# Fewer and larger stores and halo copies, transposes copied out by two engines, an earlier load of one chunk, and a divided last store in a convolution + Wave-MLP kernel

## The chip, the cores and the metric

The kernel runs on 1 core of one Trainium2 chip. The metric is the device time of one execution in microseconds (us). The engines are PE (matrix multiply, with PEld its weight loads), DVE (vector), ACT (scalar and activation), POOL (which issues the loads of input and weights) and SP (which issues stores, halo copies and row loads). In the timelines below each engine works through its own queue in order (ACT comes to a copy at 39.84 us behind three other operations), and so do the queues of DMA issues (POOL's loads of chunk 3 at 24.30 us behind the weights at 22.03).

## The reference, cut to what matters

```python
# x: (8, 4224, 192), a causal 7-tap convolution per head, then:
theta = x @ w_theta
zr, zi = x * cos(theta), x * sin(theta)
y = einsum('ts,bsd->btd', w_tok_r, zr) + einsum('ts,bsd->btd', w_tok_i, zi)
u = x + y
out = u + maximum(u @ w_ch, 0)
```

The two 4224 x 4224 token matrices are nearly all of the arithmetic. The tokens are made in 33 chunks of 128; the mixing of the first chunks has to start while later ones are still being made.

## The kernel before: the parts that the change touches

A chunk goes through `conv` (PE, from the input window `xw` with 16 rows of history from the chunk before), `transpose` (PE into PSUM tile `tp`, then a copy to `uT`), `theta` (PE, then cosine and sine on ACT), `product` and `sums` (DVE). Only then can PE mix it (`y`), and the results are added into `pv` by DVE or, on the first visit, copied by ACT.

```python
def transposed(uT, u, gs, by_dve=False):
    tp = banks("tp", F16)                      # one PSUM tile for both halves g
    for g in gs:
        for k in range(6):
            pe(nc.tensor.transpose(tp[:, g, k*P:(k+1)*P], u[:, g*GC + k*P : ...], ident))
    g = slice(gs[0], gs[-1] + 1)
    evacuate(uT[...][:, g, :], tp[:, g, 0 : 6*P], by_dve)   # ONE copy, DVE or ACT

class Chunk:
    def __init__(self, k, before=None):
        for a in range(NQ):                    # NQ = 4
            ...
            if before is not None:             # 4 halo copies of 48 KB
                nc.sync.dma_start(out=hist, in_=before.xw[lo + Q : lo + Q + HALO, h, :, :])
            ...
            nc.gpsimd.dma_start(out=self.xw[lo : lo + n, h, :, :], in_=x[:, t0 : t0 + n, :]...)
    def conv(self, j):
        ...
        if j == 1:                             # 4 stores of 96 KB, xs in token order
            for a in range(NQ):
                nc.sync.dma_start(out=xs[t0 : t0 + Q, :], in_=self.x[a*Q : (a+1)*Q, :])
    def transpose(self):
        transposed(self.xT, self.x, range(NG), self.k < 3)  # DVE for chunks 0 to 2, then ACT

def load_x(self, i):                           # x of a row block: one load of 384 KB
    nc.sync.dma_start(out=self.xr[i], in_=xs[self.tbs[i]*P : (self.tbs[i]+1)*P, :])
# ... (cut) ... in the program's start:
steps[0].load_rows()
for m in (1, 2):
    steps[0].load_w(m)       # first token weights, tile st, two buffers
load_chunk(2)
for m in (1, 2):
    steps[1].load_w(m)
for i in range(NW + 2):      # NW = 11
    # conv(i), theta(i-1), load_chunk(i + 3), transpose(i), product and sums of i-1, mixing between
```

## Time and profile before

| kernel before | value |
|---|---|
| time, median of the 4 runs beside the changed kernel | 1448.92 us (1445.77 to 1449.5) |
| span of the profiled execution | 1446.4 us |
| PE busy / PE idle | 1416.3 / 30.1 us |
| PE idle in the first 105 us, by waits | DVE accumulations 5.1 us, ACT copies 3.0 us, one late load 0.9 us |

The prediction shows the busy times, the stretches and PE's waits. These are lines of the timelines (start, duration, engine, line, operation, what it writes and reads, and in brackets the idle time before it and what ended it). An L number is a line of the kernel at hand, so the same statement has another number in another kernel.

```profile
32.85 0.96 DVE L251 TENSOR_TENSOR z<-z 128x1536 f16<-128x1536 f16 x1 [1.57 <-ACT z L246]
...
37.44 0.95 DVE L408 TENSOR_TENSOR pv<-y,pv 128x768 f32<-128x768 f32 x1
```

```profile
34.06 1.50 ACT L151 ACTIVATE uT<-tp 128x1536 f16<-128x1536 f16 x1
```

```profile
18.68 2.29 POOL L323 DMA_DIRECT2D st<-in_moe_w_tok_i_dram  x4
20.96 4.57 POOL L197 DMA_DIRECT2D xw<-in_x_dram  x8
```

DVE's accumulation at 37.44 ends PE's wait of 0.78 us at 38.45, so DVE is close to the path here.

### The profile page before, as it was taken

The numbers are of one execution on the slowest core, as the hardware profiler recorded it, in microseconds if no ns is written. First come the engines' busy times: TensorE is split into PE (matmuls) and PEld (weight loads), VectorE is DVE, ScalarE is ACT, GpSimd is POOL, SyncE is SP. The second block draws the span as 40 slices with busy tenths as digits, with TensorE's granted clock in tenths as the row PEclk, the third lists the DMA queues.
The fourth block names the chain that finished last, engine by engine and source line by source line (L and its number), as shares of the span: only waits on it lengthen the run. The fifth ranks groups of instructions, "written<-read, shape, count | busy, mean of one in ns | idle before, by whom it ended". The sixth has DMA issues, their size and how long they took to land.

```text
span 1446.4 us, 23748 instructions
## 1 busy us (share of the span) xinstructions
PE 1416.3 (98%) x9809; PEld 887.9 (61%) x9809; DVE 979.2 (68%) x1051; ACT 315.5 (22%) x379; POOL 435.1 (30%) x655
## 2 busy tenths in 40 slices
PE   7899999999999999999999999999999999999997
PEld 5556666666666666666666666666666666666665
DVE  6893555545548777866666657877777667767686
ACT  5861101111134254000000004435210110010133
POOL 7431211111233232432433342233323123213120
PEclk9999999999999999999999999999999999999999
DMA  9986756465699998998899989999999999998893
GB/s 173 227 178 145 146 103 149 90 149 97 137 231 219 214 250 217 228 254 183 213 256 213 242 143 245 228 188 234 279 216 206 209 204 221 204 203 194 166 222 125
DMA packets 272029, 281.99 MB, mean 195 GB/s; under 512 B 106672, under 2 KB 240176, under 8 KB 271920
## 3 DMA queue, kind: packets, MB, share of 16 engines
q0 software_dynamic: 162464, 92.15, 48.4%
q1 hardware_dynamic: 71824, 178.88, 35.1%
q10 hardware_dynamic: 37632, 9.44, 4.1%
q8 instruction: 77, 1.26, 0.3%
q14 instruction: 32, 0.26, 0.1%
HBM read 245.49 MB, written 108.13 MB: 244 GB/s over the span
## 4 chain that ended last, share of the span: by engine, by line
PE 89%; DVE 4%; DMA 3%; POOL 2%; ACT 1%; issue 1%; SPq 0%; DVEq 0%; ACTq 0%; POOLq 0%
PE y L443 82%; PE v L141 5%; PE pc L210 1%; PE tp L165 1%; POOL st L323 1%; DMA xw<-in_x_dram 1%; DVE z L257 1%; DVE wt L336 1%; DVE pv L408 1%; ACT z L246 1%; DVE z L251 0%; DVE pv L476 0%; DVE wt L348 0%; POOL xw L197 0%; DMA xs<-z 0%
## 5 line engine op out<-in xcount | busy, mean ns | idle before, releaser
L443 PE MATMUL y<-z,wt 128*128 128x384 f16 x7656 | 1283.6, 326 | 10.6 <-DVE pv L408 7.5
L443 PEld LDWEIGHTS <-wt 128*128 128x128 f16 x7656 | 740.8, 98 | 488.6 <-issue 10.6
L408 DVE TENSOR_TENSOR pv<-y,pv 128x768 f32<-128x768 f32 x324 | 308.9, 954 | 323.6 <-PE y L443 282.8
L336 DVE STREAM_TRANSPOSE wt<-st 128x1408 f16<-128x1408 f16 (+7 forms) x224 | 327.8, 1465 | 48.5 <-PE y L443 39.0
L323 POOL DMA_DIRECT2D st<-in_moe_w_tok_r_dram x232 | 132.5, 578 | 466.1 <-DVE wt L336 461.0
L323 POOL DMA_DIRECT2D st<-in_moe_w_tok_i_dram x232 | 132.7, 578 | 404.4 <-DVE wt L336 388.9
L348 DVE TENSOR_TENSOR wt<-wt 128x1408 f16<-128x1408 f16 (+7 forms) x216 | 176.7, 818 | 40.8 <-PE y L443 38.4
L151 ACT ACTIVATE z<-pc 128x768 f16<-128x768 f32 x65 | 53.2, 819 | 387.2 <-PE pc L210 386.9
L151 ACT ACTIVATE ub<-pv 128x768 f16<-128x768 f32 x63 | 50.2, 835 | 333.0 <-DVE pv L408 310.4
L406 ACT ACTIVATE pv<-y 128x768 f32<-128x768 f32 x66 | 54.0, 819 | 282.0 <-PE y L443 282.0
L141 PEld LDWEIGHTS <-uT 128*128 128x128 f16 x1056 | 91.0, 98 | 25.8 <-issue 7.9
L386 POOL TENSOR_TENSOR pv<-pv,xr 128x1536 f32<-128x1536 f32 x24 | 74.5, 3105 | 68.6 <-DVE pv L476 22.1
L197 POOL DMA_DIRECT2D xw<-in_x_dram x132 | 76.4, 585 | 31.0 <-DMA xw<-xw 8.7
L476 DVE SCALAR_TENSOR_TENSOR pv<-v,pv 128x768 f32<-128x768 f32 x66 | 62.9, 954 | 27.5 <-PE v L141 27.1
L257 DVE TENSOR_TENSOR z<-z 128x768 f16<-128x768 f16 x132 | 73.4, 556 | 3.6
L151 ACT ACTIVATE uT<-tp 128x1536 f16<-128x1536 f16 (+1 forms) x48 | 58.2, 1215 | 74.4 <-PE tp L165 74.4
L246 ACT ACTIVATE z<-v,half_pi 128x768 f16<-128x768 f32 x66 | 59.8, 907 | 41.2 <-PE v L141 40.8
L251 DVE TENSOR_TENSOR z<-z 128x1536 f16<-128x1536 f16 x66 | 60.0, 947 | 7.5 <-ACT z L246 7.5
L141 PE MATMUL v<-wth,uT 128*128 128x192 f16 x528 | 55.0, 248 | 4.4 <-ACT z L246 3.0
L141 PE MATMUL v<-wch,uT 128*128 128x192 f16 x528 | 54.2, 246 | 2.1 <-DVE pv L476 1.2
L246 ACT ACTIVATE z<-v 128x768 f16<-128x768 f32 x66 | 53.4, 809 | 0.0
L210 PE MATMUL pc<-xw,bands 96*64 96x192 f16 x528 | 35.8, 258 | 2.6 <-ACT bands L625 1.1
(44 smaller groups left out, 142.4 us busy)
## 6 DMA issues: line engine op xcount, KB each, us to landing
part<-pv SPq DMA_DIRECT2D x79, 768.0 KB, 4.3
pv<-part SPq DMA_DIRECT2D x79, 768.0 KB, 6.1
out_dram<-pv SPq DMA_DIRECT2D x66, 384.0 KB, 4.3
st<-in_moe_w_tok_r_dram POOLq DMA_DIRECT2D x136, 176.0 KB, 5.5
st<-in_moe_w_tok_i_dram POOLq DMA_DIRECT2D x136, 176.0 KB, 5.1
xs<-z SPq DMA_DIRECT2D x132, 96.0 KB, 4.5
xw<-in_x_dram POOLq DMA_DIRECT2D x121, 96.0 KB, 6.1
xr<-xs SPq DMA_DIRECT2D x24, 384.0 KB, 3.7
```

Of the source, the lines that this page charges most:

```text
L141: pe(nc.tensor.matmul(v[:, k, b * D : (b + 1) * D], lhsT=tT[:, 3 * k + b + i, :], rhs=w[:, 2 * b + i, :], start=(i == 0), stop=(i == 1),))
L151: act(nc.scalar.activation(out=out, in_=in_, func=AT.Copy))
L197: nc.gpsimd.dma_start(out=self.xw[lo : lo + n, h, :, :], in_=x[:, t0 : t0 + n, :].rearrange("b s d -> s b d"),)
L246: act(nc.scalar.activation(**args))
L257: dve(nc.vector.tensor_tensor(out=z[:, o, :], in0=z[:, a, :], in1=z[:, b, :], op=ALU.subtract))
L323: pool(nc.gpsimd.dma_start(out=st[a * Q : (a + 1) * Q, 0:nb, :, 0:n] .rearrange("i r bt s -> i (r bt) s"), in_=w[self.tbs[0] * P : (self.t ...
L336: dve(nc.vector.transpose(self.w[name][:, 0 : self.n, :, :], self.st[int(name[1])][:, int(name[0]) - 1, :, 0 : self.n * Q] .rearrange("p b ...
L348: dve(nc.vector.tensor_tensor(out=self.w[name][:, 0 : self.n, :, :], in0=self.w[a][:, 0 : self.n, :, :], in1=self.w[b][:, 0 : self.n, :, : ...
L386: ins = pool(nc.gpsimd.tensor_tensor(out=self.pv[i], in0=self.pv[i], in1=self.xr[i], op=ALU.add))
L408: dve(nc.vector.tensor_tensor(out=o, in0=yv, in1=o, op=ALU.add))
L443: pe(nc.tensor.matmul(y[cn][:, q, 0:BH], lhsT=self.w[wn][:, c, :, :].rearrange("p bt i -> p (bt i)"), rhs=chunks[k].z[:, zn, q * BH : (q + ...
L476: dve(nc.vector.scalar_tensor_tensor(out=ub, in0=channel_mix(self.uT[i][:, 6 * g : 6 * g + 6, :], wch), scalar=0.0, in1=ub, op0=ALU.max, o ...
```

## The change

The intent: move half of each transpose copy from ACT to DVE where ACT is busy, free SP and the DMA queues of many small issues, have chunk 2's input sooner, and shorten the end.

```diff
-    xs = dram.tile([S, N], F16, name="xs")
+    xs = dram.tile([NK, P, N], F16, name="xs")
 # transposed(): copies by halves, first ACT, then DVE
-        g = slice(gs[0], gs[-1] + 1)
-        evacuate(uT[...][:, g, :], tp[:, g, 0 : 6 * P], by_dve)
+        for g in [slice(g, g + 1) for g in gs] if shared else [slice(gs[0], gs[-1] + 1)]:
+            evacuate(uT[...][:, g, :], tp[:, g, 0 : 6 * P], shared and g.start == 1)
-            transposed(self.xT, self.x, range(NG), self.k < 3)
+            transposed(self.xT, self.x, range(NG), self.k < NW)
 # Chunk: two halo copies of 96 KB for four of 48 KB
+            for lo in (0, WR) if before is not None else ():
+                nc.sync.dma_start(out=self.xw[lo : lo + HALO, :, :, :],
+                                  in_=before.xw[lo + Q : lo + Q + HALO, :, :, :])
 # conv: one store for four
-                for a in range(NQ): ... nc.sync.dma_start(out=xs[t0 : t0 + Q, :], ...)
+                nc.sync.dma_start(out=xs[self.k, :, :], in_=self.x)
 # load_x: four loads of 96 KB for one of 384 KB
+            for j in range(NQ):
+                a, k = divmod(NQ * self.tbs[i] + j, NK)
+                nc.sync.dma_start(out=self.xr[i][j * Q : (j + 1) * Q, :],
+                                  in_=xs[k, a * Q : (a + 1) * Q, :])
 # output, last two of the kernel: ReLU-add and store by halves, on ACT's and SP's queues
+            for k in (slice(0, 1), slice(1, 2)) if last_ones else (slice(0, 2),):
+                dve(nc.vector.scalar_tensor_tensor(out=u[:, k, :], in0=v[:, k, :], ...))
+                dma = nc.scalar.dma_start if last_ones and k.start == 0 else nc.sync.dma_start
 # start of the program
     steps[0].load_rows()
+    load_chunk(2)
     for m in (1, 2):
         steps[0].load_w(m)
-    load_chunk(2)
 # (cut) the channel weights wch are loaded in a later step; the accumulating loads follow xs's new shape
```

More of the change, by code (lines that the diff above doesn't have):

```diff
@@ L133, in token, with x_rows @@
         return (a * NK + k) * Q
+    def x_rows(tb):
+        found = []
+        for j in range(NQ):
+            a, k = divmod(NQ * tb + j, NK)
+            if found and found[-1][2] == a:
+                found[-1][1].append(k)
+            else:
+                found.append((j * Q, [k], a))
+        return [
+            (slice(lo, lo + len(ks) * Q), slice(ks[0], ks[-1] + 1), slice(a * Q, (a + 1) * Q))
+            for lo, ks, a in found
+        ]
     def channel_mix(tT, w):
@@ L158, in crossed, with transposed @@
         act(nc.scalar.dma_start(out=uT, in_=u, transpose=True))
-    def transposed(uT, u, gs, by_dve=False):
+    def transposed(uT, u, gs, shared=False):
         tp = banks("tp", F16)
@@ L168, in transposed @@
                 ))
-        g = slice(gs[0], gs[-1] + 1)
-        evacuate(
-            uT[:, :, :].rearrange("p (g k) s -> p g (k s)", g=NG)[:, g, :],
-            tp[:, g, 0 : 6 * P], by_dve,
-        )
+        for g in [slice(g, g + 1) for g in gs] if shared else [slice(gs[0], gs[-1] + 1)]:
+            evacuate(
+                uT[:, :, :].rearrange("p (g k) s -> p g (k s)", g=NG)[:, g, :],
+                tp[:, g, 0 : 6 * P], shared and g.start == 1,
+            )
     Z11, T1, Z21, Z22, T2, T4, T3 = range(7)
@@ L182, in __init__ @@
             self.xw = wk.tile([2 * WR, 2, B, D], F16, name="xw", tag="big", bufs=6)
+            for lo in (0, WR) if before is not None else ():
+                nc.sync.dma_start(
+                    out=self.xw[lo : lo + HALO, :, :, :],
+                    in_=before.xw[lo + Q : lo + Q + HALO, :, :, :],
+                )
             for a in range(NQ):
@@ L185, in __init__ @@
                 t0 = token(k, a)
-                hist = self.xw[lo : lo + HALO, h, :, :]
                 if before is not None:
-                    nc.sync.dma_start(
-                        out=hist, in_=before.xw[lo + Q : lo + Q + HALO, h, :, :]
-                    )
+                    pass
                 elif t0 == 0:
-                    nc.vector.memset(hist, 0.0)
+                    nc.vector.memset(self.xw[lo : lo + HALO, h, :, :], 0.0)
                 else:
@@ L224, in conv @@
             if j == 1:
-                for a in range(NQ):
-                    t0 = token(self.k, a)
-                    nc.sync.dma_start(
-                        out=xs[t0 : t0 + Q, :], in_=self.x[a * Q : (a + 1) * Q, :]
-                    )
+                nc.sync.dma_start(out=xs[self.k, :, :], in_=self.x)
         def transpose(self):
             self.xT = turned()
-            transposed(self.xT, self.x, range(NG), self.k < 3)
+            transposed(self.xT, self.x, range(NG), self.k < NW)
         def theta(self, g):
@@ L378, in load_x @@
             self.xr[i] = wk.tile([P, N], F16, name="xr", tag="xr", bufs=1)
-            nc.sync.dma_start(
-                out=self.xr[i], in_=xs[self.tbs[i] * P : (self.tbs[i] + 1) * P, :]
-            )
+            for j in range(NQ):
+                a, k = divmod(NQ * self.tbs[i] + j, NK)
+                nc.sync.dma_start(
+                    out=self.xr[i][j * Q : (j + 1) * Q, :],
+                    in_=xs[k, a * Q : (a + 1) * Q, :],
+                )
         def add_x(self, i):
@@ L393, in add_ahead @@
             tb = self.tbs[i]
-            for cols in (slice(0, HN), slice(HN, N)):
-                pool(nc.gpsimd.dma_start(
-                    out=part[which][tb, :, cols], in_=xs[tb * P : (tb + 1) * P, cols],
-                    accum_op=ALU.add,
-                ))
+            for rows, ks, a in x_rows(tb):
+                for cols in (slice(0, HN), slice(HN, N)):
+                    pool(nc.gpsimd.dma_start(
+                        out=part[which][tb, rows, cols].rearrange("(k i) n -> i k n", i=Q),
+                        in_=xs[ks, a, cols].rearrange("k i n -> i k n"), accum_op=ALU.add,
+                    ))
         def give(self, y, i, h, copies):
@@ L473, in output @@
         def output(self, i, g):
-            u = self.pv[i][:, g * GC : (g + 1) * GC]
-            ub = u.rearrange("p (k n) -> p k n", k=2)
-            dve(nc.vector.scalar_tensor_tensor(
-                out=ub, in0=channel_mix(self.uT[i][:, 6 * g : 6 * g + 6, :], wch), scalar=0.0, in1=ub,
-                op0=ALU.max, op1=ALU.add,
-            ))
-            rows = slice(self.tbs[i] * P, (self.tbs[i] + 1) * P)
-            nc.sync.dma_start(
-                out=out[g * GB : (g + 1) * GB, rows, :].rearrange("b s d -> s b d"),
-                in_=u.rearrange("p (b d) -> p b d", d=D),
-            )
+            u = self.pv[i][:, g * GC : (g + 1) * GC].rearrange("p (k n) -> p k n", k=2)
+            v = channel_mix(self.uT[i][:, 6 * g : 6 * g + 6, :], wch)
+            rows = slice(self.tbs[i] * P, (self.tbs[i] + 1) * P)
+            last_ones = self.t == NSTEP - 1
+            for k in (slice(0, 1), slice(1, 2)) if last_ones else (slice(0, 2),):
+                dve(nc.vector.scalar_tensor_tensor(
+                    out=u[:, k, :], in0=v[:, k, :], scalar=0.0, in1=u[:, k, :],
+                    op0=ALU.max, op1=ALU.add,
+                ))
+                b = slice(g * GB + 2 * k.start, g * GB + 2 * k.stop)
+                dma = nc.scalar.dma_start if last_ones and k.start == 0 else nc.sync.dma_start
+                dma(
+                    out=out[b, rows, :].rearrange("b s d -> s b d"),
+                    in_=u[:, k, :].rearrange("p k (b d) -> p (k b) d", d=D),
+                )
         def outputs(self):
@@ L528, in step_events, with load_wch @@
                 found.append((1.3 + 3 * (m - 1), lambda m=m: nxt.load_w(m)))
+        if t == NU - 2:
+            def load_wch():
+                dve(nc.vector.memset(wch[:, 1:3, :], 0.0))
+                for rows, i, part_w in channel_pieces(moe_w_ch):
+                    pool(nc.gpsimd.dma_start(out=wch[rows, i, :], in_=part_w))
+            found.append((3, load_wch))
         for at, f in outputs:
@@ L698 @@
         between(1)
-    dve(nc.vector.memset(wch[:, 1:3, :], 0.0))
-    for rows, i, part_w in channel_pieces(moe_w_ch):
-        nc.gpsimd.dma_start(out=wch[rows, i, :], in_=part_w)
     ready[0] = NK
```

## The prediction

> **What bounds the kernel now.** I read the page first: busy times, then the chain that ended last, then the costliest group.
>
> ```profile
> PE 1416.3 (98%) x9809; PEld 887.9 (61%) x9809; DVE 979.2 (68%) x1051; ACT 315.5 (22%) x379; POOL 435.1 (30%) x655
> PE 89%; DVE 4%; DMA 3%; POOL 2%; ACT 1%; issue 1%; SPq 0%; DVEq 0%; ACTq 0%; POOLq 0%
> L443 PE MATMUL y<-z,wt 128*128 128x384 f16 x7656 | 1283.6, 326 | 10.6 <-DVE pv L408 7.5
> ```
>
> PE is busy 1416.3 of 1446.4 us, and its row also carries 89% of the chain. The token-mix matmuls (L443) are 1283.6 us of it. So the most that any change around PE can win is the 30.1 us in which PE is idle. The listing of instruction order shows that PE's own sequence is the same in both kernels, instruction for instruction: no matmul is added, removed or moved. The question is only which idle stretches of PE shrink or grow. The table of stretches tells where they lie.
>
> ```profile
> 20.00:28.00 8.00, 6.38 (x67) 4.24 (x65) 7.66 (x11) 5.19 (x7) 7.32 (x14) 1.00 1.37 196
> 28.00:39.00 11.00, 7.45 (x71) 4.66 (x67) 9.12 (x17) 8.82 (x11) 5.10 (x9) 0.99 1.32 219
> 39.00:46.00 7.00, 6.61 (x56) 4.34 (x54) 5.48 (x8) 5.56 (x7) 5.63 (x10) 0.77 0.96 133
> 46.00:63.00 17.00, 14.35 (x138) 9.69 (x139) 13.43 (x22) 15.83 (x21) 8.05 (x15) 1.00 1.28 266
> 63.00:82.00 19.00, 18.30 (x176) 12.41 (x176) 17.05 (x26) 17.86 (x24) 4.62 (x9) 1.00 1.05 225
> 82.00:105.00 23.00, 19.65 (x153) 12.70 (x152) 22.45 (x31) 13.07 (x16) 6.71 (x12) 1.00 0.82 178
> 1441.00:1446.40 5.40, 0.00 (x0) 0.00 (x0) 1.01 (x2) 0.00 (x0) 0.00 (x0) 0.89 0.50 169
> ```
>
> Columns: window, length, busy us of PE, PE weight loads, DVE, ACT, POOL, granted clock, DMA share, GB/s. Three limits follow each other in the first 105 us, where chunks are made while the mixing already runs: DMA at 20 to 28 (share over 1), ACT at 46 to 63 (15.83 of 17), DVE at 82 to 105 (22.45 of 23). After 105 PE idles only about 3 us until 1420. At the end 5.4 us pass with no PE work. The waits of PE before 110 us, in the waits view:
>
> ```profile
> PE y L443 <- DVE pv L408: 5.1, 5, 2.5
> PE y L443 <- ACT pv L406: 3.0, 3, 1.2
> PE pc L210 <- DMA xw<-in_x_dram: 0.9, 1, 0.9
> PE v L141 <- ACT uT L151: 0.8, 1, 0.8
> ```
>
> The timeline of PE dates the ones that matter:
>
> ```profile
> 27.70 0.52 PE L210 MATMUL pc<-xw,bands 96*64 96x192 f16 x7 [0.88 <-DMA xw<-in_x_dram]
> 36.31 0.48 PE L443 MATMUL y<-z,wt 128*128 128x384 f16 x2 [1.23 <-ACT pv L406]
> 38.45 0.50 PE L443 MATMUL y<-z,wt 128*128 128x384 f16 x2 [0.78 <-DVE pv L408]
> 46.45 0.83 PE L141 MATMUL v<-wth,uT 128*128 128x192 f16 x8 [0.75 <-ACT uT L151]
> 53.91 0.49 PE L443 MATMUL y<-z,wt 128*128 128x384 f16 x2 [0.61 <-ACT pv L406]
> 63.10 0.48 PE L443 MATMUL y<-z,wt 128*128 128x384 f16 x2 [0.99 <-DVE pv L408]
> 104.61 10.57 PE L443 MATMUL y<-z,wt 128*128 128x384 f16 x64 [2.46 <-DVE pv L408]
> ```
>
> [...]one record of 0.5 lasts 3.41 us from 38.87, just after the idle at 34 to 38. It costs at most 1.7 us. [...]the trace has 0.96. So I take 0.55 us for the new half of 768[...]; the next operation starts about 0.1 us before the end, which leaves 0.45 of DVE time. [...]The last store[...] 2.66 us from issue to landing, of which its 32 packets per engine of 36 ns take 1.15.
>
> **Part by part.**
>
> *Transposes on two engines, chunks 0 to 10.* Before, chunks 0 to 2 were copied whole by DVE (0.96 us), chunks 3 to 10 whole by ACT (about 1.46, next start 1.33 later). Now each is half ACT (0.81, next start 0.69 later; the same shape stands at the end of the trace) and half DVE (0.45). For chunks 3 to 10 ACT loses 0.64 each and DVE gains 0.45 each. On the path: the wait at 46.45 ends 0.65 earlier and the one at 53.91 by another 0.6, as ACT runs back to back there. So PE is about 1.25 us earlier by 58. At 36.31 ACT's saving does not count, because the next wait (38.45) is for DVE. DVE takes its halves for chunks 3 and 5 in idle time (1.57 and 1.81 us before L251). Chunk 6's half lies between L336 at 59.63 and the accumulation that ends the wait at 63.10: 0.45 back. Chunks 7 and 8 fall before an idle of 1.44 at 82.04 and are free. Chunks 9 and 10 fall into the unbroken DVE stretch that ends at 104.6: 0.9 back. About 0.4 more comes from three small ACT waits between 63 and 82. Sum: -1.25 - 0.4 + 0.45 + 0.9 = -0.3 us.
>
> *Chunk 2 loaded before the first weights.* Chunk 2 was not late (its convolution at 20.5 waits for no DMA), and the first weights move 2.3 us later: last landing near 17 instead of 14.7, while DVE needs them done by 19.7, the next transpose. Their eight instructions take 2.6 us, so that just fits. What is gained is indirect: chunk 3's halo copies can now go at about 15 us and no longer compete, at 19.6 to 21.4, with chunk 3's own loads, which land at 27.66 in a stretch with DMA share over 1. 192 KB at the 196 GB/s of that stretch is 1 us; the 0.88 us wait goes, and what follows is ACT-bound up to 38.45. I take -0.6.
>
> *Stores and halos.* Four xs stores of 0.43 us issue become one of about 0.35; four halo copies of 0.53 become two. SP saves about 2.3 us per chunk, but SP is not what PE waits for. New: the loads of x come in four pieces, and the order puts the first set between the xs stores, so SP waits at about 25 for chunk 2's store to land (4 to 5 us). Chunk 4's halos then land near 35 instead of 35.3; its convolution is at 36.7. No cost. Later the 24 loads of x issue some 1.3 us longer each; the additions that need them waited only 2.3 us in all for a load.
>
> *Channel weights later.* A memset of 0.22 leaves DVE's unbroken stretch before 104.6, and four POOL issues leave that region: -0.2.
>
> *End.* The last two ReLU-adds become four halves, each stored on its own.
>
> ```profile
> 1440.19 1.82 DVE L476 SCALAR_TENSOR_TENSOR pv<-v,pv 128x768 f32<-128x768 f32 x2 [0.91 <-PE v L141]
> 1441.17 1.23 SPq L481 DMA_DIRECT2D out_dram<-pv  x2
> ```
>
> The last full one ends at 1442.01, its store lands at 1444.70. Four halves cost DVE about 0.1 more in all; the last store carries 16 packets per engine instead of 32, so 0.58 less, while the other half has gone on ACT's queue 0.45 us before. -0.5.
>
> Sum: -0.3 - 0.6 - 0.2 - 0.5 = -1.6 us. A further -1.5 is possible if the half-clock window vanishes. [...]I count a third of it plus a little for waits that I hold too pessimistically: about -3 us in all.
>
> **The rivals.** (a) *DVE becomes the bound of the whole start.* Then its eight halves, 8 x 0.45 = 3.6 us, less 1.35 saved on chunks 0 to 2, arrive at 104.6: up to +2. For it: 22.45 of 23 us busy from 82, and the largest single wait of PE (2.46) is for DVE. Against: five idle stretches of 1.4 to 1.8 us before 82. Time: about 1450.5. (b) *A wait on SP replaces the ones removed*: x loads placed among the stores hold halos back and a chunk comes late. For it: in-order queue, DMA share over 1. Against: halos run a chunk or more ahead. Time: +2, 1451. (c) *Everything is hidden but the tail*: PE waits for other things at once, -0.5 only: 1448.7. (d) *The starting chain was as ACT- and DMA-bound as it looks* and PE recovers most of its waits and the half clock: -5, 1444.
>
> **Range and chances.** From the median before, 1449.16, less 3: **1446.0 us**. The three runs before spread over 3.7 us (1445.77 to 1449.5), and rivals lie between 1444 and 1451; weighing (a) and (b) at a fifth together, 1442.5 to 1449.8 should hold it eight times in ten. Two per cent is 29 us, which is all of PE's idle time, so faster by over 2% has 0.01; slower by as much would need a stall of that size that nothing in the profile prepares: 0.01.
>
> **What would show it.** PE busy near 1416 us and the same instruction counts. The wait at 27.7 for in_x_dram gone or under 0.3. No PE wait for the ACT transpose copy near 46. DVE busy about 2.3 us more in total, and PE's wait before 105 us still for the accumulation, at 2 us or more. ACT below 14.5 of 17 us in 46 to 63. The last two stores landing 0.5 us nearer to the last DVE instruction. Wrong would be: PE reaching its long unbroken run (104.6 now) later than 105, a new wait for the halo copies or for xs, or a changed idle total between 105 and 1420, which I take to be untouched.

The sum stays at -1.6 us, and at about -3 with a third of 1.5 for the half clock and some 0.9 for waits. What is missing is the working of the 0.55 us for DVE's half copy, from which the 0.45 of the first step comes, so 0.55 stands as the author's guess beside the 0.96 of a whole copy; the trace before shows 0.556 us for DVE's subtractions of 128x768 in f16 (`z<-z`, L257, mean of 132), and the half copies of the changed kernel then took 0.56 (L163). The 1.5 rests on the record alone, 3.41 us at a granted clock of 0.5; what brings such a record about was not shown.

## More of the kernel before

ACT's whole transpose copy starts at 34.06, after DVE's product at 32.85: in this kernel DVE never waits for that copy. And POOL issues chunk 3's loads from 20.96, right behind the second set of weights.

## The result, and the profile after

| | before | after |
|---|---|---|
| time, median of 4 runs | 1448.92 us (1445.77 to 1449.5) | 1461.93 us (1458.39 to 1463.47) |
| ratio of the fast runs, 95% interval | | 1.0091 (1.0067 to 1.0115) |
| span of the profiled execution | 1446.4 us | 1461.2 us |
| PE busy | 1416.3 us | 1421.4 us |
| PE idle | 30.1 us | 39.8 us |

A ratio here is the mean time of one kernel's fast runs over that of the other's of the same rounds, so not quite the ratio of the medians quoted beside it. The change costs about 13 us, or 0.9%: within 2%, but 12 us above the predicted range.

In the profiled executions the span grew by 14.8 us, and that is PE idle +9.7 and PE busy +5.1. The first line is from the page's busy times and the second from its costliest groups (busy us, mean ns of one; idle before it).

```profile
PE 1421.4 (97%) x9809; PEld 889.8 (61%) x9809; DVE 981.3 (67%) x1061; ACT 313.0 (21%) x382; POOL 437.7 (30%) x657
...
L459 PE MATMUL y<-z,wt 128*128 128x384 f16 x7656 | 1287.5, 327 | 14.9 <-DVE pv L424 13.3
```

There are 9809 matmuls as before and in the same order, so a longer busy time points to a slower clock: the mean granted clock is 0.993 in place of 0.998, and the table of stretches below shows where. The idle time before the mixing matmuls for a DVE accumulation went from 7.5 to 13.3 us. The timeline of PE dates the new waits:

```profile
32.03 0.85 PE L226 MATMUL pc<-xw,bands 96*64 96x192 f16 x7 [3.34 <-DMA xw<-in_x_dram]
...
47.16 0.82 PE L459 MATMUL y<-z,wt 128*128 128x384 f16 x2 [4.39 <-DVE pv L424]
...
117.09 5.30 PE L459 MATMUL y<-z,wt 128*128 128x384 f16 x16 [3.24 <-DVE pv L424]
```

Against the same matmuls before (27.70, 38.45 and 104.61), PE is 4.3 us late at 32, 8.7 us late at 47 and 12.5 us late at 117; by 122.5 it is 15.1 us late, and from there to the end the difference stays at 15. Between 47 and 117 it grows mostly in two waits, of 1.19 us for a DVE accumulation at 68.99 and of 1.36 us for ACT at 89.02.

Where the 4.39 us come from is seen on DVE, ACT and PE's transposes together:

```profile
33.70 0.70 DVE L348 STREAM_TRANSPOSE wt<-st 128x512 f16<-128x512 f16 x1
40.69 0.56 DVE L163 COPY uT<-tp 128x768 f16<-128x768 f16 x1 [6.28 <-ACT uT L165]
...
46.16 0.95 DVE L424 TENSOR_TENSOR pv<-y,pv 128x768 f32<-128x768 f32 x1
```

```profile
37.66 0.90 ACT L258 ACTIVATE z<-v,half_pi 128x768 f16<-128x768 f32 x1 [0.35 <-PE v L155]
38.46 0.80 ACT L258 ACTIVATE z<-v 128x768 f16<-128x768 f32 x1
39.15 0.81 ACT L422 ACTIVATE pv<-y 128x768 f32<-128x768 f32 x1
39.84 0.82 ACT L165 ACTIVATE uT<-tp 128x768 f16<-128x768 f16 x1
```

```profile
37.78 0.83 PE L179 MATMUL tp<-ident,z 128*128 128x128 f16 x12
```

DVE stood still for 6.28 us, from 34.4 to 40.69, until ACT had copied *its* half of the same chunk; and ACT came to that half only after a cosine, a sine and an accumulator copy that stood ahead in its queue. Not all of the 6.28 us is ACT's: PE's transposes of this chunk, late like the chunk itself, ended at 38.61, and only the last 2.08 us passed after that. The product, the sums and the accumulation that PE waits for stand behind DVE's half in DVE's queue, so all of them were held, by both. The view of waits sums this up for the first 125 us (us in total, times, longest):

```profile
DVE uT L163 <- ACT uT L165: 17.1, 7, 6.3
```

Set against the ends of PE's transposes, about 9.7 of the 17.1 us passed after the transposes were done, and the rest before. The trace says why ACT comes last each time: the one semaphore that these copies of DVE wait for is ACT's. Both copies read one PSUM tile, and in this kernel as built its two readers on different engines come one after the other.

The 3.34 us at 32 start on POOL:

```profile
12.94 0.58 POOL L335 DMA_DIRECT2D st<-in_moe_w_tok_r_dram  x1 [1.12 <-DMA xw<-in_x_dram]
...
18.53 2.29 POOL L335 DMA_DIRECT2D st<-in_moe_w_tok_r_dram  x4 [2.74 <-DVE wt L348]
22.03 2.29 POOL L335 DMA_DIRECT2D st<-in_moe_w_tok_i_dram  x4 [1.21 <-DVE wt L348]
24.30 5.70 POOL L213 DMA_DIRECT2D xw<-in_x_dram  x10
```

The second weights need a free buffer, hence DVE's transposes of the first; these come later because the first weights come later (last landing 20.16 us, before 14.71). Chunk 3's loads stand behind the second weights in POOL's queue: from 24.30 in place of 20.96, landing at 31.98 in place of 27.66.

The slower clock shows in the table of stretches (columns as in the prediction: the number after POOL's is the granted clock, the share of PE's full clock that it was given; half clock is 0.5):

```profile
30.00:38.00 8.00, 5.97 (x41) 4.19 (x42) 4.27 (x7) 4.16 (x6) 4.44 (x9) 0.57 1.38 201
44.00:51.00 7.00, 3.83 (x22) 2.36 (x23) 6.43 (x12) 1.70 (x3) 1.92 (x4) 0.51 0.09 10
115.00:123.00 8.00, 5.91 (x20) 2.88 (x21) 5.93 (x8) 0.00 (x0) 2.29 (x4) 0.57 0.44 59
```

Each of these three stretches holds a half-clock record of 6.83 us (from 30.55, 44.21 and 115.89), each beside one of the three waits above. Before there was one, of 3.41 us from 38.87 (a record after PE's last matmul, in both kernels, is left out). Compared matmul by matmul, all of the 5.1 us of added busy time lies in the three records. So the waits are paid twice here: once as idle time (9.7 us more), and once as matmuls at half speed (5.1 us more; in the kernel before, eight theta matmuls take 0.83 us at 28.15 and 1.40 at 38.79, where the record begins). The runs agree: of the four executions after, the one with a mean granted clock of 0.996 took 1458.39 us and the two with 0.993 took 1462.94 and 1463.47.

At the end of the kernel, the last store still needs 2.68 us from issue to landing (2.66 before).

### The profile page after: what moved, and what is told of

Its sections match the earlier page's. It is cut to its first block, busy times and chain, and to the rows that moved or that the text cites. A ratio compares the mean times of both kernels' runs of the same rounds, so it can differ in the third digit from the quotient of the medians.

```text
span 1461.2 us, 23581 instructions
## 1 busy us (share of the span) xinstructions
PE 1421.4 (97%) x9809; PEld 889.8 (61%) x9809; DVE 981.3 (67%) x1061; ACT 313.0 (21%) x382; POOL 437.7 (30%) x657
## 4 chain that ended last, share of the span: by engine, by line
PE 90%; DVE 6%; ACT 2%; issue 1%; DMA 1%; POOL 0%; DVEq 0%; ACTq 0%; POOLq 0%
PE y L459 82%; PE v L155 5%; PE pc L226 2%; DVE z L269 1%; PE tp L179 1%; DVE z L263 1%; DVE pv L424 1%; ACT z L258 1%; DVE wt L348 1%; DVE wt L360 1%; DVE pv L495 0%; ACT uT L165 0%; DMA st<-in_moe_w_tok_r_dram 0%; DMA xw<-xw 0%; DMA wsb<-in_weight_dram 0%
## 5 line engine op out<-in xcount | busy, mean ns | idle before, releaser
L459 PE MATMUL y<-z,wt 128*128 128x384 f16 x7656 | 1287.5, 327 | 14.9 <-DVE pv L424 13.3
L459 PEld LDWEIGHTS <-wt 128*128 128x128 f16 x7656 | 741.7, 98 | 495.5 <-issue 12.5
L401 POOL TENSOR_TENSOR pv<-pv,xr 128x1536 f32<-128x1536 f32 x24 | 74.5, 3104 | 79.5 <-DMA xr<-xs 38.2
L495 DVE SCALAR_TENSOR_TENSOR pv<-v,pv 128x768 f32<-128x768 f32 (+1 forms) x68 | 63.0, 930 | 26.4 <-PE v L155 25.9
L165 ACT ACTIVATE uT<-tp 128x768 f16<-128x768 f16 (+1 forms) x51 | 55.5, 1089 | 76.5 <-PE tp L179 76.5
```

The costliest lines, as they stand in the source:

```text
L165: act(nc.scalar.activation(out=out, in_=in_, func=AT.Copy))
L401: ins = pool(nc.gpsimd.tensor_tensor(out=self.pv[i], in0=self.pv[i], in1=self.xr[i], op=ALU.add))
L459: pe(nc.tensor.matmul(y[cn][:, q, 0:BH], lhsT=self.w[wn][:, c, :, :].rearrange("p bt i -> p (bt i)"), rhs=chunks[k].z[:, zn, q * BH : (q + ...
```

## The experiments

Eighteen kernels ran; each came out correct. The kernel before, run beside them on the same chip, stood between 1446.3 and 1452.5 us, so differences of one or two us between medians are at the edge of what these runs resolve.

| run | what it is | median us | before, same set | ratio (95%) |
|---|---|---|---|---|
| e1 | after, order of first loads back | 1457.95 | 1449.04 | 1.0065 (1.0048-1.0081) |
| e2 | after, whole transpose copies back | 1454.96 | 1449.04 | 1.0036 (1.0019-1.0053) |
| e3 | after, both back | 1450.91 | 1449.04 | 1.0013 (0.9998-1.0028) |
| e4 | before + order alone | 1449.30 | 1449.04 | 1.0002 (0.9987-1.0016) |
| e5 | before + split alone, ACT first | 1458.61 | 1450.19 | 1.0064 (1.0047-1.0080) |
| e6 | e5 with a PSUM tile per half | 1458.57 | 1450.19 | 1.0063 (1.0048-1.0078) |
| e7 | e5 with DVE first | **1447.46** | 1450.19 | 0.9987 (0.9972-1.0002) |
| e8 | e3, x loads held back by a wait | 1455.46 | 1450.19 | 1.0050 (1.0007-1.0094) |
| e9 | after with DVE first | 1451.1 (3 fast runs) | 1449.66 | 1.0016 (1.0001-1.0031) |
| e10 | before + divided end alone | 1449.84 | 1449.66 | 1.0000 (0.9988-1.0013) |
| e11 | before + merged halo copies alone | 1449.14 | 1449.66 | 0.9997 (0.9985-1.0010) |
| e12 | e7 again | **1447.17** | 1449.66 | 0.9985 (0.9969-1.0000) |
| e13 | after, x of a row block in one load | 1508.48 | 1448.94 | 1.0419 (1.0397-1.0440) |
| e14 | e3, x in one load | 1501.22 | 1448.94 | 1.0372 (1.0350-1.0395) |
| e15 | after, order back, DVE first, x in one load | 1502.73 | 1448.94 | 1.0353 (1.0322-1.0384) |
| e16 | after, DVE first, x in one load | 1503.54 | 1448.94 | 1.0382 (1.0363-1.0400) |
| e17 | after, order back, DVE first, x stores and loads in program order | 1450.06 | 1449.42 | 1.0010 (0.9996-1.0023) |
| e18 | e17 with the order as changed | 1452.53 | 1449.42 | 1.0028 (1.0014-1.0041) |

### Undoing one part at a time (e1 to e4)

Theories at this point: A, the order of the first loads starts a chain of lateness; B, the split copies hold DVE; C, the x loads in pieces stand among the first stores in SP's queue and hold halo copies.

e1 is the changed kernel with

```diff
     steps[0].load_rows()
-    load_chunk(2)
     for m in (1, 2):
         steps[0].load_w(m)
+    load_chunk(2)
```

> The changed kernel with one part undone: chunk 2 is loaded after the first weights again. Theory A (the load order is the cause: first weights land 4 us later, so the staging buffers come free later, chunk 3 arrives 4.3 us later, PE idles 3.3 us there and falls to half clock): PE's wait for chunk 3's load falls from 3.3 to under 1.5 us, and the kernel is at 1452 us or less, at least 8 us faster than the changed one. Theory B (the split transposes are the cause: DVE's half waits for ACT's half, and everything behind it on DVE waits too): only 3 to 5 us faster than the changed kernel, 1456 to 1459; DVE still waits some 10 us in all for ACT's half. Theory C (the x loads in pieces hold up SP's queue): no change, 1460 or more.

e2 is the changed kernel with the whole copies of before (`transposed` and its call as before), e3 with both, and e4 is the kernel before with only the order changed.

> The changed kernel with the transposes whole again (chunks 0 to 2 by DVE, the others by ACT), chunk 2 still loaded first. Theory A: chunk 3 is as late as in the changed kernel, PE's wait for its load stays near 3 us, at most 4 us faster, 1457 or more. Theory B: the 4.4 us wait of PE for DVE's accumulation near 47 us goes below 2, and the kernel is at 1453 or less. Theory C: no change.

> The changed kernel with load order and whole transposes as before; stores, halos, x loads in pieces, channel weights later and the split end stay. If A and B together are the whole cause: at the kernel before or 0.5 to 1.5 us below it (1447 to 1449), the 0.5 being the end. Theory C (x loads in pieces or the new store layout): still 1453 or more, with a PE wait for halo copies.

> The kernel before with chunk 2's load moved ahead of the first weights and nothing else. Theory A: 1455 or more, PE's wait for chunk 3's load above 3 us and at least one record of half clock more. Theory B: within 2 us of the kernel before, as whole transposes on ACT never hold DVE.

Measured: 1457.95, 1454.96, 1450.91 and 1449.30. Taking the split out is worth 7.0 us in both pairs (1461.93 - 1454.96 and 1457.95 - 1450.91); taking the order back is worth 4.0 us in both (1461.93 - 1457.95 and 1454.96 - 1450.91). So neither A nor B is the whole. The order alone on top of the kernel before costs 0.3 us, with an interval of some 2 us either way, though in its profile PE waits 1.54 us at 29.94 for chunk 3 (0.88 before). With both back, 1.9 us remain by the medians; the interval (0.9998 to 1.0028) also allows no cost at all. The timeline of PE in e3 shows a wait that fits C:

```profile
29.23 0.24 PE L226 MATMUL pc<-xw,bands 96*64 96x192 f16 x1 [2.91 <-DMA xw<-xw]
30.85 0.56 PE L226 MATMUL pc<-xw,bands 96*64 96x192 f16 x7 [1.38 <-DMA xw<-in_x_dram]
```

Chunk 3's halo copies (`xw<-xw`) were issued at 23.02 and 23.64 (before: 19.56 to 21.43), behind a piece of x that waited in SP's queue until 22.61 for a store of x to land.

### The split by itself, and which engine goes first (e5 to e7)

e5 is the kernel before plus the split alone. e6 gives each half its own tile (and, unlike e5, also copies chunks 11 to 32 in halves, both by ACT):

```diff
-            transposed(self.xT, self.x, range(NG), self.k < 3)
+            for g in range(NG):
+                tp = banks("tp", F16)          # a tile per half
+                for k in range(6): pe(nc.tensor.transpose(tp[:, g, ...], ...))
+                tps.append(tp)
+            for g in range(NG):
+                evacuate(uT half g, tps[g][:, g : g + 1, 0 : 6 * P], self.k < NW and g == 1)
```

e7 changes one number of e5:

```diff
-                tp[:, g, 0 : 6 * P], shared and g.start == 1,
+                tp[:, g, 0 : 6 * P], shared and g.start == 0,
```

> The kernel before with one part of the change alone: the transposes of chunks 0 to 10 evacuated in halves, ACT first, then DVE. Theory S (the halves run one after the other, because both read one PSUM tile; DVE, in order, stands still behind ACT's half, and everything DVE does for chunks and weights is late): the 7.0 us that taking the split out recovered in both pairs so far come back alone: 1455 to 1457 us, ratio 1.004 to 1.006, with DVE waits for ACT's half copy (uT) of 8 us or more in all before 110 us, and PE waiting over 1 us for a DVE accumulation near 40 to 47. Rival I (the split hurts only together with the reordered loads or the early x loads): 1448 to 1451, ratio within 0.999 to 1.001. Rival D (DVE's added 8 x 0.45 us of work itself, not the wait): at most 2 us, 1449 to 1451.

> As the run before it, but each half has a PSUM tile of its own, so DVE's half waits for PE alone (the instruction listing shows this). It costs a second buffer of the pool of two for each chunk. Theory S: DVE's waits for ACT's half copy are gone, and most of the 7 us with them: 1448 to 1451, if the second buffer does not make PE wait instead; a PE wait on buffer release that takes the place would leave 1451 to 1455. Rival D (DVE's added work is the cost): as slow as the run with one tile, 1455 to 1457.

> As the split alone, with one number changed: DVE takes the first half and ACT the second, so that ACT waits for DVE and DVE for nobody but PE. Same work on both engines, same buffers. Theory S: DVE's waits for ACT's half copy are gone; ACT may wait 0.5 us for DVE; 1447 to 1451, at least 4 us below the split with ACT first. Rival D (added DVE work): no difference to the split with ACT first, 1455 to 1457.

Measured: 1458.61, 1458.57 and 1447.46. The split alone costs 8.4 us (1458.61 - 1450.19), a little more than the 7 expected. The same work with DVE first costs nothing and is 11.1 us faster than with ACT first. That rules out the added work on DVE as the cause (rival D): DVE does the same eleven half copies in both. The line of DVE that carries it, in e5 and then in e7, each with the accumulation that follows:

```profile
36.16 0.56 DVE L149 COPY uT<-tp 128x768 f16<-128x768 f16 x1 [2.68 <-ACT uT L151]
...
41.22 0.95 DVE L408 TENSOR_TENSOR pv<-y,pv 128x768 f32<-128x768 f32 x1
```

```profile
32.72 0.56 DVE L149 COPY uT<-tp 128x768 f16<-128x768 f16 x1 [1.59 <-PE tp L165]
...
37.78 0.95 DVE L408 TENSOR_TENSOR pv<-y,pv 128x768 f32<-128x768 f32 x1
```

In e7 DVE takes its half as soon as PE has made it, and the accumulation comes 3.4 us earlier. PE's wait for it is 1.56 us in place of 3.98. DVE's waits at these copies fall from 16.8 us, of which 11.0 passed after PE's transposes were done, to 7.2, all for PE. ACT now waits for DVE (7.7 us in all before 125 us), and PE waits 1.4 us in all for ACT's half. In e7 no half-clock record is left before the end; e5 has one of 6.83 us and one of 3.41.

e6 missed its expectation in an instructive way. The wait on ACT is gone from DVE, as Theory S said, but the time is not. The timeline of PE shows what came in its place:

```profile
34.40 0.49 PE L237 MATMUL tp<-ident,z 128*128 128x128 f16 x6 [1.41 <-ACT z L259]
...
41.00 0.82 PE L456 MATMUL y<-z,wt 128*128 128x384 f16 x2 [3.13 <-DVE pv L421]
```

The two tiles use up both buffers of their pool, so PE's second six transposes wait until ACT has read the theta result out of the other buffer: ten such waits, 11.8 us in all. DVE's half then waits for those transposes (15.2 us for PE, in place of 16.8 for ACT). One wait was exchanged for another of the same size. Before 125 us no wait of DVE for ACT's half copy is left in e6 (16.8 us in e5), though the halves are still copied by the two engines, and the result is correct. So it is the one tile that orders the readers, in the kernel as built.

### The x loads held, and DVE first in the whole change (e8, e9)

e8 is e3 with a dependence that holds each x load behind the DVE instruction ahead of it in the program; e9 is the changed kernel with the one number of e7.

> The changed kernel with the order of the first loads and the whole-transpose copies as before (measured 1450.9 against 1449.0 before), and with the loads of x held behind the DVE instruction that precedes them in the program, so that they no longer go among the first stores of x. Theory C (x pieces in SP's queue wait for a store of x to land and hold the halo copies of chunk 3 behind them): halo copies of chunk 3 are issued by 21 us and not at 23, PE's wait of 2.9 us at 29 us for halo copies is gone or under 0.5, time 1447.5 to 1449.5. Rival T (the remaining cost lies in DMA traffic or elsewhere): 1450 to 1452, with the wait at 29 us still 2 us or more.

> The whole changed kernel with one number changed: DVE evacuates the first half of each transposed chunk and ACT the second, so that DVE waits only for PE. With the split as the only change, this one number took 11.1 us off (1458.6 to 1447.5). Theory S (DVE standing behind ACT's half is what the split costs, in the whole change too): at least 7 us off the changed kernel's 1461.9, so 1449 to 1455, DVE's waits for ACT's half copy gone and PE's wait for the DVE accumulation near 47 us under 2 us; what stays over 1449 is the order of the first loads with the early x loads (4 us by the earlier pair). Rival R (in the whole change the late loads set the pace and the order of the halves does not matter): under 3 us off, 1459 to 1462.

e8 has two results. Early, the halo wait of 2.9 us is gone as theory C said, but chunk 3's own loads then end the wait (2.28 us at 29.39). Later, until 608.57, PE waits 2.22 us for an accumulation of DVE, which waits 5.75 us for POOL's addition, which has waited 5.37 us for the load of x that SP now holds. Its four runs spread from 1451.43 to 1465.66, so holding SP was a bad tool, and the time says nothing about C.

e9 behaved as Theory S expected: 1451.1 us, which is 10.8 us below the changed kernel's 1461.93. Its profiled execution fell into a slow state (1961.97 us, with a mean granted clock of 0.709), so that trace isn't compared; the time is that of the other three runs.

### The end, the halos, and DVE first once more (e10 to e12)

e10 is the kernel before with the new `output` alone, e11 with the merged halo copies alone. e12 repeats e7, the split with DVE first on the kernel before; its label names the end as well, but the end is not in it.

> The kernel before with the end of the change alone: the last two ReLU-adds in halves, each half stored by itself, on the queues of ACT and SP. Prediction's step: the last store carries half the packets and lands about 0.5 us earlier after the last DVE instruction: ratio 0.9995 to 0.9997 of before, which the spread of 3 us between runs may not resolve; in the profile the time from the last DVE instruction to the end falls from 3.4 us to 2.9 or less. Rival Q ([...]the last half lands no sooner): last store 2.6 to 2.7 us from issue to landing as before, end within 0.2 us, ratio 0.9990 to 1.0010.

> The kernel before with the halo copies alone changed: two per chunk of 96 KB in place of four of 48 KB. The first copy of a chunk now waits for loads of both column halves of the chunk before it. If merged halos are part of the 1.9 us that the stores, halos and x loads cost together: 1450 to 1451, with chunk 2 or 3 waiting for a halo copy. If they are harmless and the early x loads or the one large store are the cause: 1448 to 1450, ratio within 0.9990 to 1.0010 and PE's wait near 27.7 us still for chunk 3's own load and under 1.2 us.

> A repeat in another set of runs of the split alone with DVE taking the first half (1447.5 against 1450.2 before, ratio 0.9987 with an interval from 0.9972 to 1.0002), as a base for a best version. If the gain is real: ratio 0.997 to 0.9995, 1445.5 to 1448.5. If it was the spread of the runs: ratio 0.9995 to 1.001.

The end alone gives 1.0000 and the halos alone 0.9997: neither is part of the cost, and neither gains what can be seen. In e10's profile the last store takes 2.37 us from issue to landing in place of 2.66, and from the last DVE instruction to that landing 2.40 in place of 2.69; the four half operations cost DVE 1.95 us in place of 1.82. That leaves about 0.15 us. e12 confirms e7: 1447.17 against 1449.66.

### One x load per row block (e13 to e16)

All four replace the four pieces by one load over the same rows:

```diff
-            for j in range(NQ): ... xr[j*Q : (j+1)*Q, :] <- xs[k, a*Q : (a+1)*Q, :]
+            for rows, ks, a in x_rows(self.tbs[i]):
+                nc.sync.dma_start(out=self.xr[i][rows, :],
+                                  in_=xs[ks, a, :].rearrange("k i n -> k i n"))
```

> The whole changed kernel, only the x of a row block is loaded by one transfer in place of four pieces. The listing shows that its first x load then stands after the stores of ten chunks and no longer among those of the first three. Theory C (x pieces stand in SP's in-order queue, wait for a store of x and hold back halo copies and later stores; this is what makes the earlier load of chunk 2 cost 4 us and adds part of the 1.9): 1461.9 less 3 to 6, that is 1456 to 1459; PE's wait for chunk 3 at 32 us down from 3.3 to about 1.5 (what the order alone showed). Rival P (the order costs its 4 us by POOL issuing chunk 3's loads 3.3 us later, whatever SP does): 1460 to 1463, wait at 32 us still 3 us or more.

> The changed kernel with the order and the whole-transpose copies as before (1450.9 measured, 1.9 over before), and one x load per row block. Held behind a DVE instruction, the pieces cost more later in the run (1451 to 1466). Theory C: PE's wait of 2.9 us at 29 us for halo copies is gone, 1448 to 1449.5, ratio 0.999 to 1.0005. Rival B[...]: halo wait gone but chunk 3's own loads land at 29 us or later and PE waits 1.5 us or more for them; 1450 to 1452.

> The candidate: the changed kernel with chunk 2 loaded after the first weights as before, DVE taking the first half of each transposed chunk, and one x load per row block. Split with DVE first alone gave 1447.2 and 1447.5 against 1449.7 and 1450.2; tail and merged halos alone gave 1.0000 and 0.9997. If the costs are understood and no other is left: 1446 to 1448.5, ratio 0.9975 to 0.9995. If the single store costs by itself: 1448.5 to 1450.5.

> As the candidate, but with chunk 2 loaded before the first weights, as the change has it; against the candidate only the order differs. Theory C (the order costs only with the x pieces): within 1 us of the candidate, 1446.5 to 1449.5. Rival P (the order costs by itself, through POOL's later issues): 2 to 4 us over the candidate, 1449.5 to 1452.5, with PE waiting over 1.5 us for chunk 3's loads.

All four missed, by some 50 us. In e14 the early part went as theory C said (no halo wait; the matmul that waited until 29.23 in e3 runs at 26.34), but from 600 us on POOL's additions wait 89.2 us in all for x. Such a load issued at 598.18 let its addition start at 608.42, ten us later, where the whole load before took a median of 3.7 us. The traces show how the two loads differ: in e14 the 128 packets of the load issued at 598.18 (3072 bytes each) took 6.9 us, with more than four in flight for only 0.1 us of it; those of a whole load in the kernel before (issued at 594.18) took 1.9 us, with twelve or more in flight for 1.1 us of it. Why fewer packets of the new load go at once was not shown. These runs answer nothing about the change, whose pieces have 32 rows each.

### Place in the queue fixed, nothing else (e17, e18)

```diff
-                nc.sync.dma_start(out=xs[self.k, :, :], in_=self.x)
+                sp(nc.sync.dma_start(out=xs[self.k, :, :], in_=self.x))
 # and the same sp(...) around each piece of load_x: program order on SP, no wait added
```

> The changed kernel with chunk 2 loaded after the first weights as before, DVE taking the first half of each transposed chunk, and SP's stores and loads of x kept in program order, with no wait added: the listing shows the first x pieces behind the stores of the first ten chunks and behind those of the middle. If the costs are understood: PE waits under 1 us for halo copies near 29 us, no loss in the middle of the run, 1446 to 1448.5, ratio 0.9975 to 0.9995, as the split with DVE first alone (1447.2, 1447.5). If the single store or the pieces cost by themselves, even in place: 1448.5 to 1451.

> The same with chunk 2 loaded before the first weights, as the change has it. Theory C (the order costs only with x pieces in front of halo copies): within 1 us of the run before it. Rival P (the order costs by itself, through the weights and through POOL's later issues for chunk 3): 2 to 4 us over it, with PE waiting 1.5 us or more for chunk 3's own loads near 30 us. The run with the pieces early stood at 1452.1.

Measured: 1450.06 and 1452.53. The pieces now stand behind the stores of ten chunks, and the halo wait is gone. Still the medians of these two runs of one set differ by 2.5 us for the order. Their times overlap (1449.63 to 1453.03 and 1450.77 to 1456.09), so it is the profiles (of the slowest execution of each) that speak for rival P and against theory C as an account of the order's cost: without any wait for a halo copy PE idles 32.7 us in e18 and 29.8 in e17, and waits longer for chunk 3's own loads. The two timelines of PE, e17 and e18:

```profile
28.68 0.52 PE L229 MATMUL pc<-xw,bands 96*64 96x192 f16 x7 [0.90 <-DMA xw<-in_x_dram]
```

```profile
31.92 0.52 PE L229 MATMUL pc<-xw,bands 96*64 96x192 f16 x7 [2.75 <-DMA xw<-in_x_dram]
```

The chain is the one seen in the changed kernel. With the order changed, the first weights land by 20.64 in place of 14.73; DVE waits 4.6 us for them (no such wait in e17); POOL, waiting for the buffer, issues the first of the second imaginary weights at 22.52 in place of 19.26 and chunk 3 from 24.79 in place of 22.05; its four loads land by 31.88 in place of 28.63. Why the same order costs only 0.3 us on the kernel before (e4, with a wait of 1.54 us) stays open.

e17 was the candidate and does not beat the kernel before. Against e7 and e12 (ratios 0.9987 and 0.9985), its 1.0010 leaves some 3 us to the single store, the x pieces, the later channel weights, or all three. In the profiled executions PE is busy 1421.5 us in e17 and 1415.6 in e12 with the same matmuls, while it idles 29.8 and 29.3 us. So the difference is half clock there (records of 3.41, 6.83 and 3.41 us, none in e12 before the end); but the execution profiled for e17 was its slowest (1453.03). Which of the three parts brings the half clock stays open. The best version is the kernel before with the split and DVE first (e7, e12): 1447.2 to 1447.5 us against 1449.7 to 1450.2, some 2.5 us better, with intervals that end at 1.0002 and 1.0000. Little of the gain is less waiting: PE idles 30.7 us in e7's profile, 29.3 in e12's and 30.1 in the kernel before, but neither e7 nor e12 has the half-clock record of 3.41 us. Five executions of the kernel before that kept a granted clock of 1.000 took 1446.74 to 1447.78, as e7 and e12 do.

## Why the prediction was wrong, point by point

- **The total and the sign.** Predicted 1446.0 us (1442.5 to 1449.8), measured 1461.93. That the time stays within 2% was right. Of the 3 us, some 0.9 (beyond the sum of 1.6 and a third of 1.5) had no working. The sum of separate effects is: order of the halves 10.8 us (after against e9), order of the loads 2.5 (e18 against e17), stores and the like some 3.5 (0.0024 of 1449, e17 against e7 and e12), less 2 us that the split gains with DVE first. That is 14.8 against the 13.0 measured; the terms are each known to a us or two and share waits.
- **"Transposes on two engines", the step that failed most.** Its sum was -0.3 us; alone it measured +8.4. The durations were right: the half copy took DVE 0.56 us (taken as 0.55). Other signs came true without showing much. DVE's total rose by 2.1 us (predicted 2.3), but with the same work on DVE it reads 979.0 in e5, 980.5 in e7 and 981.0 in e12. ACT was busy 12.86 of 17 us between 46 and 63 (under 14.5), in a stretch that holds earlier work than before, as PE is 8.7 us late. PE's wait of 0.75 us near 46 for ACT's copy is gone, but the same matmul, at 55.31, now waits 0.77 us for DVE's half. What failed was "DVE takes its halves for chunks 3 and 5 in idle time": the working gave each half a duration and no wait. DVE's half could not start before ACT's had ended, and ACT reached its half late: 16.8 us of DVE waits in e5, 17.1 in the whole change, where 0 was counted. Rival (a) named DVE as a bound, but for its 3.6 us of added work; e7 shows that the work itself costs nothing.
- **"Chunk 2 loaded before the first weights."** It took -0.6 us with the first weights landing "near 17", which "just fits" before 19.7. They landed at 20.16. The missing terms were how long the eight weight transfers take behind chunk 2's four, with the DMA share at 1.49 from 12 to 17 us (2.3 us were allowed for four more issues; the last landing came 5.4 us later), and that chunk 3's loads stand behind the second weights in POOL's queue, which wait for DVE to free the first. In place of a gain, 2.5 to 4 us inside the change (0.3 on the kernel before). The halo copies did go at 14.59 and 15.34, as foretold, and that gained nothing. "The wait at 27.7 gone or under 0.3" became 3.34 at 32.
- **"Stores and halos: no cost."** Rival (b) named the x pieces, and in e3 they did hold halo copies (2.91 us). That its +2 is so near the +1.9 of e3 may well be luck: the interval there allows no cost at all, in the whole change PE waits for no halo copy, and with the pieces out of the way (e17) the cost stayed. Later, POOL's additions waited 38.2 us in all for x in place of 2.3, at no cost to PE, whose lateness stays at 15 us.
- **The half clock.** The text counted a third of a gain of 1.5 us. The profile went the other way: from one record of 3.41 us to three of 6.83, and PE busy +5.1 us where "near 1416" was the test. It goes with waits, but not with their sum: e7 idles as long as the kernel before and has no record before the end. Nor did a record before the end follow a wholly idle stretch of 3.41 us in the two kernels compared here: of the 3.41 us before each record, PE had idled 1.6 us in the kernel before (from 35.46), and 1.9, 2.0 and 2.0 us in the changed one. What brings a record about was not shown.
- **"End", -0.5.** Measured 1.0000 alone, and about 0.15 us in its profile. In the whole change the last store landed no sooner (2.68 us).
- **"Channel weights later", -0.2.** Not tried alone.
- **Between 123 and 1420 us** nothing changed, as predicted.

## What to carry to other kernels

When work on one tile is divided between two engines, look for a wait between the two copies, and let the engine go first whose queue holds the work that the bound engine waits for; durations alone don't show this (the order of the halves was worth 11.1 us, e5 against e7). When a load is moved ahead, follow what it pushes back through every in-order queue to the next load behind it (here chunk 3's, issued from 24.30 in place of 20.96 us). And waits of some us on PE can cost more than their length (here 5.1 us of half clock on top of 9.7 us of idle time), so a sum of waits should allow for matmuls at half clock.
